# A delta-rule attention block and a GELU feed-forward in one kernel: small steps move between ScalarE, GpSimd, VectorE and the DMA queues

## The chip, the cores and the metric

The kernel runs on one core of a Trainium2 chip. A core has TensorE (matrix products into PSUM), VectorE, ScalarE and GpSimd (called DVE, ACT and POOL in the profile) and SyncE (SP), which here only issues DMAs. Each engine works through its own queue in order and waits on semaphores where it needs another's result. The metric is the device time of one execution in microseconds; the kernel before has a median of 678.57 us in 6 runs (676.61 to 679.24).

## The reference, cut to what matters

```python
# batch 4, heads 8, seq 768, head dim 48; everything float32
k_n = k / (norm(k) + 1e-6)
for t in range(seq):
    y[t]  = q[t] @ state                       # read before the update
    v_old = k_n[t] @ state
    state = state + beta[t] * outer(k_n[t], v[t] - v_old)

x   = y as (4*768, 8*48)                       # 3072 tokens of 384
h   = x @ w_in                                 # 384 -> 2048
out = (0.5 * h * (1 + erf(h / sqrt(2)))) @ w_out   # 2048 -> 384
```

`w_in` and `w_out` arrive as float64 (a division by a NumPy square root made them so); the kernel turns them into float32 itself.

## The kernel before, in words

**Tiling.** The sequence is cut into 12 chunks of 64 steps. A chunk is held as two units (`a` = 0, 1), each with two batches on the two halves of the 128 partitions and 8 heads along the free side. A unit's number within a pair of chunks is `u.t` = 0 to 3; `first` are the four units of chunks 0 and 1, `third` the two of chunk 2, `fourth` the two of chunk 3.

**Attention.** Within a chunk the recurrence becomes a triangular system per head. For a pair of chunks ("group" 0 holds chunks 0 and 1, group 1 chunks 2 and 3, and so on) the kernel

- squares K and sums per head (`squares`, L272), takes the root (`root` for group 0, a power instruction on GpSimd in `prep`, L303, later) and makes factors from beta and the norm (`factors`, L264; `finish_both`, `finish`);
- forms products of K with K (`grams`, `diagonals`) and of Q with K (`queries`; for chunks from 2 on VectorE applies the causal mask while it reads PSUM, L396);
- inverts the 32 by 32 diagonal blocks on VectorE: a scaled mask XM on GpSimd (L423), a flip (L428, L429), some 30 elimination steps (L436, L438), and transposes back (L447, L451);
- joins the 32 blocks into blocks of 64 on TensorE in two levels (`join`, `join_run`, L511), with VectorE scaling level 0 (L519) and ScalarE copying level 1 (L523).

Then each chunk in turn is put against the state (psK, L566; W, L574), solved (psU), used (psY) and transposed to `xT` for the feed-forward. V is multiplied by K's norm first (`scale_v`, L326, on GpSimd).

**Feed-forward.** A chunk has 16 blocks of the first layer (`fc1`: psH, L671; GELU on ScalarE, L673). The second layer is psO (L684) with a copy on ScalarE (L688) and two output DMAs from ScalarE's queue (L678) for chunks 0 and 1, and a scheme with fewer products (L709) for the others. psH and psO share two PSUM banks (tag `mlp`), so a psH has to wait until the GELU, or the psO copy, two before it has read its bank. The tag `dn` has two buffers as well, which psG, psJ, psK, psU and psY take in the order in which the program asks for them.

**Weights.** The 16 parts of `w_in` and `w_out` are unpacked from float64 bits by five VectorE instructions each (`begin`, `mantissas`, `signed`: L219 to L237) with one exponent pass on ScalarE (`exponents`, L224). The raw bits wait in memory that is used otherwise later.

**Order.** Up to L899 the order on every engine is written by hand. After that each step has a plan time: chunk c's feed-forward lies from c + 1 to c + 2, and the other steps are put at times between (`at`, L790). All are sorted by plan time and emitted. VectorE executes in exactly that order; for the other engines a planner goes through the emitted instructions with estimated costs, and takes the earliest emitted one that is ready when an engine is free. What it decides is fixed in the program; on the chip each engine executes its list in order.

**What the change touches.** The beta DMAs (L163, on GpSimd's queue) and K's and Q's first loads (L152, L155); the hand-written loop over `first` (L823 to L830) with beta's transposes (`signs`, L802); `squares` and `prep` (L272 to L303), where chunks 2 and 3 take one ScalarE instruction per head with an accumulated sum (L280); `scale_v` (L325); the zeroing of `Kb`, a padded K buffer of later chunks (L911); and plan times in L920 to L935. `Kb` lies in the memory of the closed start pool, so it can be written only after the last unpacking.

Of the kernel before, what the change touches and what calls it, by code (L numbers as in the profile page):

```python
# [8 lines left out]
F32 = mybir.dt.float32  # L9
# [3 lines left out]
ACT = mybir.ActivationFunctionType  # L13
# [3 lines left out]
def kernel(  # L17
# [133 lines left out]
    for u in first:  # L151
        fetch_in(u.Kp[:, :, 0:D], k, u, (nc.sync, nc.scalar))  # L152
    bt = w_in_sb.rearrange("q g m f -> q (g m f)")[0:B * H, 0:2 * S].rearrange(
        "n (c p t) -> n c p t", p=2, t=C)
    for u in first:  # L155
        fetch_in(u.Qp[:, :, 0:D], q, u)
# [6 lines left out]
    for p in range(2):  # L163
        nc.gpsimd.dma_start(out=bt[:, :, p, :],
                            in_=beta.rearrange("b h (c t) -> (b h) c t", t=C))
# [106 lines left out]
    def squares(u, n, engine=None):  # L272
        kd = u.Kn[:, :, 0:D]
        if engine is nc.gpsimd:
            ksq = su.tile([128, H, D], F32, tag="w_e", name="ksq")
        else:
            ksq = wk.tile([128, H, D], F32, tag="ksq", name="ksq")
        if engine is None and u.c < 4:
            for h in range(H):
                nc.scalar.activation(ksq[:, h], kd[:, h], ACT.Square, accum_out=n[:, h:h + 1])  # L280
            return
        if engine is None:
            nc.scalar.activation(ksq, kd, ACT.Square)
        else:
            engine.tensor_tensor(ksq, kd, kd, op=ALU.mult)
        nc.vector.tensor_reduce(n, ksq, axis=AX.X, op=ALU.add)  # L286

    def prep(c):
        us = [tiles[c, a] for a in range(NA)]
        g = c // 2  # L290
        if c % 2 == 0:
            new_group(g)
        if c == 2:
            n23 = wk.tile([128, 2 * NA, H], F32, tag="n0", name="n0", bufs=1)
            ns[2], ns[3] = n23[:, 0:NA], n23[:, NA:]
            ns["both"] = n23
        elif c > 3:
            ns[c] = wk.tile([128, NA, H], F32, tag="n", name="n", bufs=4)
        n = ns[c]
        for u in us:  # L300
            squares(u, n[:, u.a])
        flat = n.rearrange("q a h -> q (a h)")
        nc.gpsimd.tensor_tensor(flat, flat, half, op=ALU.pow)  # L303
# [21 lines left out]
    def scale_v(u, engine=nc.gpsimd):  # L325
        engine.tensor_tensor(u.V, u.V, ns[u.c][:, u.a].unsqueeze(2).to_broadcast([128, H, D]),  # L326
                                op=ALU.mult)
# [495 lines left out]
    for u in first:  # L823
        squares(u, n0[:, u.t], nc.gpsimd if u.t % 2 else nc.vector)
        transposed(u, (0,))
        if u.t > 0:
            diagonals(first[u.t - 1])
        if u.t == 2:
            signs(0, 2)
# [75 lines left out]
    def late():  # L905
        start.close()
        more.append(ctx.enter_context(tc.tile_pool(name="late", bufs=1)))
        small[0] = ctx.enter_context(tc.tile_pool(name="few", bufs=1, space=bass.MemoryType.PSUM))
        for a in range(NA):
            Kb = more[0].tile([128, 2, NP, 2, HB], F32, name=f"Kb{a}")  # L910
            nc.gpsimd.memset(Kb, 0.0)  # L911
            for c in range(5, NC, 2):
                tiles[c, a].Kb = Kb
# [6 lines left out]
    plan += [at(0.99, 1.0, [(1.0, prep, 2)]), at(1.65, 1.655, [(1.0, finish_both)]), at(2.75, 2.76, [(1.0, finish, 4)]), at(2.45, 2.46, [(1.0, queries, third)]),  # L920
             at(1.12, 1.6, state_steps(1)), at(1.45, 1.46, [(1.0, prep, 3)]),
             at(1.75, 2.45, eliminate_steps(1)),
             at(2.58, 2.74, join_steps(1)), at(2.72, 2.98, state_steps(2)),
             at(2.6, 2.61, [(1.0, prep, 4)]), at(2.8, 2.9, [(1.0, grams, [tiles[4, a] for a in range(NA)])])]
# [3 lines left out]
    for c in range(4, NC):  # L928
# [5 lines left out]
        t = c - (2.1 if c % 2 == 0 else 2.6) if c > 5 else {4: 2.1, 5: 2.62}[c]  # L934
# [62 lines left out]
```

## Time and profile before

| what | value |
|---|---|
| median of 6 runs | 678.57 us (676.61 to 679.24) |
| the profiled execution | 681.93 us |
| its span, first to last instruction | 679.9 us |
| mean granted TensorE clock | 0.975 |
| TensorE busy (matmul) | 647.5 us, 95% |
| VectorE busy | 450.9 us, 66% |
| ScalarE busy | 220.9 us, 32% |
| GpSimd busy | 90.2 us, 13% |
| share of TensorE in the chain that ended last | 75% |

How to read it: times in the profile count from the span's start. A row of a timeline has the start in us, the duration in us, the engine, the source line, the operation, output and inputs by their names in the program, the shapes, how often (x24: 24 neighbours merged), and in brackets how long the engine had been idle before and what released it. "issue" stands for a wait that the profile can't put down to anybody. PEld is TensorE loading weights, which overlaps its matmuls. A float32 matmul appears as two instructions, so a block of psH is six.

### The profile page before, as it was taken

The numbers are of one execution on the slowest core, as the hardware profiler recorded it, in microseconds if no ns is written. First come the engines' busy times: TensorE is split into PE (matmuls) and PEld (weight loads), VectorE is DVE, ScalarE is ACT, GpSimd is POOL, SyncE is SP. The second block draws the span as 40 slices with busy tenths as digits, with TensorE's granted clock in tenths as the row PEclk, the third lists the DMA queues.
The fourth block names the chain that finished last, engine by engine and source line by source line (L and its number), as shares of the span: only waits on it lengthen the run. The fifth ranks groups of instructions, "written<-read, shape, count | busy, mean of one in ns | idle before, by whom it ended". The sixth has DMA issues, their size and how long they took to land.

```text
span 679.9 us, 21674 instructions
## 1 busy us (share of the span) xinstructions
PE 647.5 (95%) x9542; PEld 564.6 (83%) x9542; DVE 450.9 (66%) x920; ACT 220.9 (32%) x571; POOL 90.2 (13%) x91
## 2 busy tenths in 40 slices
PE   6867999998999999999999999999999999999997
PEld 4655875775689988989989989989989989989996
DVE  5999899895589865569856569856569844324021
ACT  3357654212443033233142233142142133132220
POOL 5051300402211012111021111021111010000000
PEclk9976799997999999999999999999999999999999
DMA  9785646202532142421233421221301210100101
GB/s 129 182 239 171 121 122 174 47 0 44 89 46 40 40 54 52 68 52 26 50 44 54 71 47 25 48 27 28 58 13 25 53 20 3 24 2 2 23 1 25
DMA packets 157566, 39.75 MB, mean 58 GB/s; under 512 B 149216, under 2 KB 152288, under 8 KB 157472
## 3 DMA queue, kind: packets, MB, share of 16 engines
q1 hardware_dynamic: 151424, 33.06, 25.5%
q10 hardware_dynamic: 5952, 5.12, 3.4%
q8 instruction: 75, 1.23, 0.8%
q0 software_dynamic: 96, 0.20, 0.1%
q14 instruction: 19, 0.16, 0.1%
HBM read 33.62 MB, written 4.72 MB: 56 GB/s over the span
## 4 chain that ended last, share of the span: by engine, by line
PE 75%; DVE 5%; issue 1%; POOL 0%; ACT 0%
PE psH L671 31%; PE psY L709 12%; PE psX L709 12%; PE psZ L709 4%; PE psJ L511 3%; PE psK L566 3%; PE psG L361 3%; PE psO L684 2%; PE psU L591 2%; DVE tmp L436 2%; PE psY L609 2%; DVE Nu L438 2%; PE psY L618 1%; PE psX L653 1%; DVE u L754 0%
## 5 line engine op out<-in xcount | busy, mean ns | idle before, releaser
L671 PE MATMUL psH<-xT,w_in_sb 128*128 128x256 f32 x1152 | 264.0, 386 | 3.9 <-ACT G L673 3.2
L671 PEld LDWEIGHTS psH<-xT,w_in_sb 128*128 128x128 f32 x1152 | 217.8, 192 | 35.7 <-ACT G L673 4.4
L673 ACT ACTIVATE G<-psH 128x256 f32<-128x256 f32 x192 | 73.3, 383 | 189.7 <-PE psH L671 177.8
L438 DVE TENSOR_TENSOR Nu<-Nu,tmp 128x30 f32<-128x30 f32 (+9 forms) x180 | 62.3, 346 | 6.2
L436 DVE TENSOR_TENSOR tmp<-Nu 128x30 f32<-128x30 f32 (+9 forms) x180 | 61.6, 342 | 5.1
L709 PE MATMUL psY<-w_out_sb,G 128*128 128x192 f32 x320 | 57.0, 329 | 1.1 <-DVE u L754 0.4
L709 PE MATMUL psX<-w_out_sb,G 128*128 128x192 f32 x320 | 56.2, 329 | 0.0
L709 PEld LDWEIGHTS psY<-w_out_sb,G 128*128 128x128 f32 x320 | 51.7, 190 | 2.8 <-DVE u L754 2.5
L709 PEld LDWEIGHTS psX<-w_out_sb,G 128*128 128x128 f32 x320 | 52.2, 190 | 0.7
L684 PE MATMUL psO<-w_out_sb,G 128*128 128x384 f32 x128 | 47.3, 512 | 0.2 <-DVE w_out_sb L237 0.2
L654 ACT COPY xT<-psX 128x384 f32<-128x384 f32 x24 | 11.4, 478 | 106.7 <-PE psX L653 105.5
L303 POOL TENSOR_TENSOR n<-n,half 128x16 f32<-128x16 f32 x10 | 29.4, 2941 | 92.6 <-DVE n L286 69.1
L597 ACT COPY U<-psU 64x192 f32<-64x192 f32 x96 | 30.0, 313 | 19.6 <-PE psU L591 18.4
L396 DVE TENSOR_TENSOR P<-psG,mask 128x1024 f32<-128x1024 f32 x10 | 12.3, 1228 | 35.9 <-PE psG L361 35.9
L684 PEld LDWEIGHTS psO<-w_out_sb,G 128*128 128x128 f32 x128 | 23.7, 196 | 14.1 <-DVE w_out_sb L237 0.9
L326 POOL TENSOR_TENSOR V<-V,n 128x384 f32<-128x384 f32 x22 | 22.0, 1009 | 95.3 <-DMA V<-in_v_dram 41.6
L574 DVE TENSOR_TENSOR W<-psK,V 128x384 f32<-128x384 f32 x22 | 12.2, 552 | 33.4 <-ACT y L573 33.4
L460 POOL MEMSET Zf<- 32x512 f32 x23 | 12.4, 540 | 153.5 <-DVE Zf L451 125.0
L718 DVE TENSOR_TENSOR S<-G 128x512 f32<-128x512 f32 x20 | 13.8, 688 | 25.8 <-ACT G L673 25.7
L632 DVE TENSOR_TENSOR x<-psY,y 64x192 f32<-64x192 f32 x80 | 28.2, 353 | 0.9
L709 PE MATMUL psY<-T,G 128*128 128x192 f32 x160 | 28.2, 329 | 0.0
L709 PE MATMUL psX<-T,G 128*128 128x192 f32 x160 | 28.1, 329 | 0.0
(135 smaller groups left out, 860.5 us busy)
## 6 DMA issues: line engine op xcount, KB each, us to landing
Kp<-in_k_dram SPq DMA_DIRECT2D x76, 96.0 KB, 3.5
w_out_sb<-in_moe_w_in_dram SPq DMA_DIRECT2D x24, 256.0 KB, 3.9
V<-in_v_dram SPq DMA_DIRECT2D x48, 96.0 KB, 2.9
out_dram<-o_sb ACTq DMA_DIRECT2D x48, 96.0 KB, 2.2
w_raw<-in_moe_w_out_dram SPq DMA_DIRECT2D x10, 384.0 KB, 4.3
Zf<-in_moe_w_out_dram SPq DMA_DIRECT2D x6, 384.0 KB, 4.4
Qp<-in_q_dram SPq DMA_DIRECT2D x64, 32.0 KB, 2.1
Qp<-in_q_dram SPq DMA_DIRECT2D x16, 96.0 KB, 4.6
```

Source lines behind the costliest of these rows:

```text
L303: nc.gpsimd.tensor_tensor(flat, flat, half, op=ALU.pow)
L326: engine.tensor_tensor(u.V, u.V, ns[u.c][:, u.a].unsqueeze(2).to_broadcast([128, H, D]), op=ALU.mult)
L361: nc.tensor.matmul(psG[HALF[p], r, i * NP + j, :], lhsT=u.Kt[rows, p, j, :], rhs=(u.Qt if x else u.Kt)[rows, p, j, :], start=True, stop=True)
L436: nc.vector.tensor_tensor(tmp, nu[:, j + 1:, j:j + 1].to_broadcast([128, n, j]), nu[:, j:j + 1, 0:j].to_broadcast([128, n, j]), op=ALU.mult)
L438: nc.vector.tensor_tensor(nu[:, j + 1:, 0:j], nu[:, j + 1:, 0:j], tmp, op=ALU.add)
L511: nc.tensor.matmul(psJ[to, i, :], lhsT=(xm if level else off)[rows, u, :], rhs=zf[rows, u, HB:C] if level else xm[rows, u, :], start=True, ...
L597: copy(pairs(u.U[HALF[p]], s), u.psU[HALF[p ^ s], p])
L632: nc.vector.tensor_tensor(dst, src, pairs(u.y[HALF[p ^ s]], s), op=ALU.add)
L671: nc.tensor.matmul(psH, lhsT=w_in_sb[:, f // 2, m, f % 2 * 128:(f % 2 + 1) * 128], rhs=xTs[c][:, m, :], start=(m == 0), stop=(m == NM - 1))
L673: nc.scalar.activation(G[:, f, :], psH, ACT.Gelu)
L684: nc.tensor.matmul(u.psO, lhsT=G[:, f, u.a * 128:(u.a + 1) * 128], rhs=w_out_sb[:, f, :], start=(f == 0), stop=(f == NF - 1))
L709: nc.tensor.matmul(ps_, lhsT=lhs[:, f, :], rhs=rhs[:, f, :], start=first and f == 0, stop=f == FH - 1, skip_group_check=not first)
```

## The change

- **Beta.** Its two DMAs go to SyncE's queue, behind K and ahead of Q, instead of GpSimd's.
- **The hand-written start.** The squares of unit 3 are done by VectorE instead of GpSimd; `diagonals` of unit 2 comes after the loop; beta's transposes (`signs(0, 2)`) come after it instead of after unit 2's transposes.
- **Squares of chunks 2 and 3.** The same 32 ScalarE instructions, formerly inside `prep(2)` (plan time 0.99) and `prep(3)` (1.45), are single steps with plan times from 1.08 to 1.5. Both `prep`s, now holding only the power instruction for these chunks, are at 1.51.
- **V of chunks 2 and 3.** Eight ScalarE multiplies per unit, one per head with the norm as a scale per partition, instead of one GpSimd instruction per unit.
- **Kb.** Zeroed by ScalarE (a mask times 0.0) instead of a GpSimd memset.
- **Plan times around the joins of group 1.** The masked queries of chunk 2 move from 2.45 to 2.675 and `prep(4)` from 2.6 to 2.67, both behind the second of the three joins (2.58 to 2.74); `finish(4)` moves from 2.75 to 2.97; the load of chunk 5's K from 2.62 to 2.69.

```diff
     for u in first:
         fetch_in(u.Kp[:, :, 0:D], k, u, (nc.sync, nc.scalar))
...
+    for p in range(2):
+        nc.sync.dma_start(out=bt[:, :, p, :], in_=beta.rearrange("b h (c t) -> (b h) c t", t=C))
     for u in first:
         fetch_in(u.Qp[:, :, 0:D], q, u)
...
-    for p in range(2):
-        nc.gpsimd.dma_start(out=bt[:, :, p, :],
-                            in_=beta.rearrange("b h (c t) -> (b h) c t", t=C))
...
-        if engine is None and u.c < 4:
-            for h in range(H):
-                nc.scalar.activation(ksq[:, h], kd[:, h], ACT.Square, accum_out=n[:, h:h + 1])
-            return
...
+    def sum_of_squares(u, h):
+
+        if "both" not in ns:
+            n23 = wk.tile([128, 2 * NA, H], F32, tag="n0", name="n0", bufs=1)
+            ns[2], ns[3] = n23[:, 0:NA], n23[:, NA:]
+            ns["both"] = n23
+        if h == 0:
+            u.ksq = wk.tile([128, H, D], F32, tag="ksq", name="ksq")
+        nc.scalar.activation(u.ksq[:, h], u.Kn[:, h, 0:D], ACT.Square,
+                             accum_out=ns[u.c][:, u.a, h:h + 1])
...
     def scale_v(u, engine=nc.gpsimd):
+        if u.c in (2, 3):
+            for h in range(H):
+                nc.scalar.mul(u.V[:, h], u.V[:, h], ns[u.c][:, u.a, h:h + 1])
+            return
...
     for u in first:
-        squares(u, n0[:, u.t], nc.gpsimd if u.t % 2 else nc.vector)
+        squares(u, n0[:, u.t], nc.gpsimd if u.t == 1 else nc.vector)
         transposed(u, (0,))
-        if u.t > 0:
-            diagonals(first[u.t - 1])
-        if u.t == 2:
-            signs(0, 2)
+        if u.t in (1, 2):
+            diagonals(first[u.t - 2 + 1])
+    diagonals(first[2])
+    signs(0, 2)
     diagonals(first[3])
...
-            nc.gpsimd.memset(Kb, 0.0)
+            nc.scalar.mul(Kb.rearrange("q p j h n -> q (p j h n)"),
+                          low.rearrange("q a b -> q (a b)")[:, 0:NP * 4 * HB], 0.0)
...
-    plan += [at(0.99, 1.0, [(1.0, prep, 2)]), at(1.65, 1.655, [(1.0, finish_both)]), at(2.75, 2.76, [(1.0, finish, 4)]), at(2.45, 2.46, [(1.0, queries, third)]),
-             at(1.12, 1.6, state_steps(1)), at(1.45, 1.46, [(1.0, prep, 3)]),
+    sums = [(1.0, sum_of_squares, tiles[c, a], h) for c in (2, 3) for a in range(NA) for h in range(H)]
+    plan += [at(1.08, 1.5, sums), at(1.51, 1.511, [(1.0, prep, c) for c in (2, 3)]), at(1.65, 1.655, [(1.0, finish_both)]), at(2.97, 2.971, [(1.0, finish, 4)]), at(2.675, 2.676, [(1.0, queries, third)]),
+             at(1.12, 1.6, state_steps(1)),
...
-             at(2.6, 2.61, [(1.0, prep, 4)]), at(2.8, 2.9, [(1.0, grams, [tiles[4, a] for a in range(NA)])])]
+             at(2.67, 2.671, [(1.0, prep, 4)]), at(2.8, 2.9, [(1.0, grams, [tiles[4, a] for a in range(NA)])])]
...
-        t = c - (2.1 if c % 2 == 0 else 2.6) if c > 5 else {4: 2.1, 5: 2.62}[c]
+        t = c - (2.1 if c % 2 == 0 else 2.6) if c > 5 else {4: 2.1, 5: 2.69}[c]
```

## The prediction

> **What bounds the kernel now.** I read the page's rows of busy time first, then busy time by stretch (cut where the work changes its kind), then each engine's own timeline around the edits. The stretches, with their columns PE, PEld, DVE, ACT, POOL, clock, DMA share, GB/s:
>
> ```profile
> PE 647.5 (95%) x9542; PEld 564.6 (83%) x9542; DVE 450.9 (66%) x920; ACT 220.9 (32%) x571; POOL 90.2 (13%) x91
> ```
>
> ```profile
> 0.00:43.00 43.00, 30.62 (x721) 25.38 (x723) 33.72 (x94) 18.66 (x38) 11.83 (x26) 0.96 0.88 195
> ...
> 96.00:123.50 27.50, 27.08 (x158) 16.61 (x157) 26.91 (x39) 10.29 (x20) 2.49 (x4) 1.00 0.58 153
> 123.50:187.00 63.50, 57.74 (x810) 41.59 (x809) 43.89 (x97) 18.14 (x43) 13.96 (x12) 0.95 0.28 48
> 187.00:680.00 493.00, 487.22 (x7005) 443.70 (x7003) 298.73 (x630) 138.39 (x344) 47.34 (x40) 1.00 0.21 35
> ```
>
> TensorE is busy 487 of the last 493 us and waits for nobody there, so what the change wins or loses before 187 us arrives at the end one for one. Up to 121 us VectorE is the bound: it unpacks the weights (L219 to L237), 26.91 of 27.50 us busy, and the second matmul of chunk 0 (psO) can't run ahead of the last unpacked part. From 123 to 187 the two take turns.
>
> **Squares of chunks 2 and 3 (ScalarE).** TensorE's timeline:
>
> ```profile
> 64.20 1.56 PE L671 MATMUL psH<-xT,w_in_sb 128*128 128x256 f32 x6
> 67.95 1.61 PE L671 MATMUL psH<-xT,w_in_sb 128*128 128x256 f32 x6 [2.19 <-ACT G L673]
> ...
> 71.35 7.81 PE L671 MATMUL psH<-xT,w_in_sb 128*128 128x256 f32 x24
> ...
> 81.10 5.45 PE L671 MATMUL psH<-xT,w_in_sb 128*128 128x256 f32 x24
> ```
>
> Thirteen squares run from 64.6 to 67.5 on ScalarE ahead of the first GELU; both psH banks are full, and TensorE idles 2.19 us. Then the same 24 matmuls take 7.81 instead of 5.45 us, and the 64 small ones of L478 1.92 instead of 1.20: half clock, 2.4 + 0.7 = 3.1 us. Given late plan times the squares yield to a GELU that is ready; a GELU then waits for one square (0.23 us each). I count the bubble and the half clock after it as gone: TensorE is 2.2 + 3.1 = 5.3 us ahead at 79 us.
>
> Here a rule weighs in. The Trainium skill, "TensorE: Matmul & The Clock Gate", section "HAM oscillation", lets the clock fall only after idle gaps above about 3.4 us. By it a gap of 2.19 us costs itself alone, the slow stretch stays, and the stall that I find below has no clock penalty. The row says otherwise: a fresh gap of 2.19 us, then half speed. Over this trace, a stretch of 3.4 us that is about half idle is followed by slow matmuls; 1.47 us of idle at 150.6 was not. I take the row.
>
> What is this worth? TensorE may not overtake the unpacking. VectorE, though, twice waits for others in this stage, and a third time just after it:
>
> ```profile
> 80.88 0.56 DVE L574 TENSOR_TENSOR W<-psK,V 128x384 f32<-128x384 f32 x1 [2.26 <-ACT y L573]
> ...
> 91.81 0.96 DVE L236 SCALAR_TENSOR_TENSOR w_e<-Zf,w_e 128x768 uint32<-128x768 uint32 x1 [1.10 <-ACT w_e L224]
> ...
> 125.49 1.83 DVE L429 TENSOR_TENSOR Nu<-Nu,XM 128x1024 f32<-128x1024 f32 x1 [1.62 <-POOL XM L423]
> ```
>
> The first waits for psK, which follows seven blocks of psH on TensorE; 5.3 us earlier, the wait of 2.2 is gone. The second is an exponent pass (L224) queued behind eight copies of U (2.6 us); with TensorE ahead these come before the pass is due: 1.1. So the unpacking ends **3.3 us** earlier; 1.7 if the half clock stayed, and near nothing if ScalarE were late elsewhere. The other 2 us of TensorE's lead turn into idle, harmlessly. Both power instructions (L303, 2.9 us each) on POOL move behind the last square; the norms are wanted at 120.7, so even a delay of 15 us is covered.
>
> **Start.** POOL loses two beta DMAs (1.44 us), SP gains them behind K: at its 0.7 us per issue, 1.4 us for every later load on SP (Q, V, w_in, next K and Q). I find at least 2 us between landing and use for each, so this is free; without that cover it is 1.4. The beta transfer (96 packets between 4.2 and 7.4 us) leaves K's transfers alone, the last tile's squares go to VectorE (0.55 us instead of a wait of 1.29 for POOL), and the beta transposes move one tile later. VectorE's root starts up to 1.1 us sooner, but the flip of the diagonals needs the last diagonal, which TensorE's stall of 1.14 us at 12.4 holds. Between 0 and 1.1 I take **0.5**.
>
> **V and Kb leave POOL.** POOL's timeline:
>
> ```profile
> 121.01 1.00 POOL L911 MEMSET Kb<- 128x512 f32 x2 [38.60 <-PE psG L361]
> 121.96 1.63 POOL L326 TENSOR_TENSOR V<-V,n 128x384 f32<-128x384 f32 x2
> 123.53 1.92 POOL L423 TENSOR_TENSOR XM<-low,gt 128x1024 f32<-128x1024 f32 x1
> ```
>
> Without the first two, XM starts at 122.0, and VectorE's elimination 1.5 us earlier.
>
> But ScalarE now does two zeroings (the row of L458, half a microsecond apart: 1.1) and 16 multiplies for chunk 2, with plan times below those of the copies of psO (L688). All become ready at the end of the unpacking, D; L688 only 1.6 us later, so ScalarE is taken. A multiply of 128x48: the square's row says 0.23, its start-to-start without the accumulator's read 0.14 is the lower end. The Trainium skill, "ScalarE: Activation LUTs", section "What ACT_TABLE_LOAD costs", adds about 93 ns for a scale read per partition, and lets neighbours overlap by as much: an estimate of 0.32 each, 0.23 apart. I take 0.23: 3.6 us (2.2 to 5.1). With 0.14 the sum would end 1.4 us lower.
>
> ```profile
> 122.46 0.48 ACT L688 COPY o_sb<-psO 128x384 f32<-128x384 f32 x1 [5.86 <-PE psO L684]
> ...
> 123.55 2.75 PE L671 MATMUL psH<-xT,w_in_sb 128*128 128x256 f32 x12
> 127.02 5.23 PE L671 MATMUL psH<-xT,w_in_sb 128*128 128x256 f32 x23 [0.71 <-ACT G L673]
> ```
>
> L688 starts at D + 4.9 instead of D + 1.6; behind it in ScalarE's queue stand the output DMAs and the first GELUs, and psH of chunk 1 has no bank before the copy. The second psH pair, and all after it, starts **3.3 us** later relative to D. About 2.7 of it is one gap, over half of a 3.4 us stretch: by the reading above half clock follows, **2.5 us** of matmul time. Chunk 3's 16 multiplies rank below the GELUs and fill gaps of 0.9 us between them.
>
> **Joins in front of the mask.** The same place on VectorE, then on TensorE:
>
> ```profile
> 155.27 1.25 DVE L396 TENSOR_TENSOR P<-psG,mask 128x1024 f32<-128x1024 f32 x1
> 156.39 1.04 DVE L286 TENSOR_REDUCE n<-ksq 128x8 f32<-128x384 f32 x2
> 157.46 1.39 DVE L519 TENSOR_TENSOR XM<-psJ,gm 32x512 f32<-32x512 f32 x2
> ```
>
> ```profile
> 156.57 0.24 PE L511 MATMUL psJ<-XM,G 32*32 32x32 f32 x2 [0.56 <-DVE P L396]
> 158.95 0.23 PE L511 MATMUL psJ<-Zf,XM 32*32 32x32 f32 x1 [2.13 <-issue]
> ```
>
> L519 moves ahead of 2.0 us of work, so with the 1.5 above it comes 3.5 us earlier. The late "issue" wait ends 0.1 us after L519, which frees its PSUM bank: a wait on VectorE. The 128 query matmuls (psG, 1.1 us), now in the gaps of 113 to 121, move here and add 1.1.
>
> From 127.0 to 186.3 (chunk 2's first psH) TensorE takes 59.3 us. Of it 1.47 + 0.56 + 2.13 + 0.27 + 0.62 = 5.05 are idle, and 1.9 half clock after 158 (four psO take 2.93, two 1.39, where two take 0.91 later). Pure work 52.4, plus 1.1: 53.4. With VectorE's chain ahead it runs unbroken: 3.3 + 2.5 + 53.4 = 59.2. This stretch thus gains **0.1**; five microseconds of idle are spent on the stall. Moving finish(4), prep(4), a K load (four issues on SP, between block loads) by some hundredths of a chunk happens while VectorE has gaps of 5 and 8 us: nothing, and at worst their own 1.8 us.
>
> **Sum.** 0.5 + 3.3 + 0.1 = 3.9 us. The profiled execution took 681.93 (span 679.9, 2.0 around it), so 678.0 in its terms; on the median 678.57, **674.7**. A measurement of this kernel can tell about 0.2%, 1.4 us, from no change.
>
> **Rivals.**
> - *No stall for chunk 1, or a short one without half clock.* For it: the stall rests on an order that the planner decides and on a price no row shows exactly. With the stall and full clock 2.5 us less: 672.2. With no stall, TensorE waits 0.9 us for the joins, and the stretch ends 4.2 earlier: 670.6. Middle 671.5.
> - *The unpacking keeps its pace.* ScalarE then delays the exponents behind squares: gain only 0.5 + 0.1, 678.0: no change. Against it: L224 has 3.8 us from L219 to L236, and squares are short.
> - *Slower: ScalarE's multiplies hold psH.* If the 32 multiplies of both chunks stand ahead of L688 at 0.32 us each (10.2 + 1.3), it starts 9.9 us later: 6.6 beyond my sum, 681.3. It decides from a shift of 3.3 + 3.9 = 7.2 us. Against it: chunk 3's plan times (2.6) lie above L688's (1.9).
>
> **Chances.** My sum 0.44; no or little stall 0.32; unpacking unchanged 0.10; slower 0.14. So faster 0.76, same 0.10, slower 0.14. The range, 670.0 to 680.0, reaches over the first three and the unknown price of a multiply, and leaves the last out.
>
> **What would show it.** Right: no wait of psH for a GELU near 66, 24 psH in 5.5 us after it; L574 without a wait; the last L237 of the unpacking at about 117; L429 straight behind L428; 16 ScalarE multiplies ahead of L688, then a TensorE gap over 2 us and slow psH; no gap over 1 us at the joins. Wrong: L688 ahead of the multiplies (faster), the last L237 still at 120 (no gain), or beta's transposes waiting for their DMA and the elimination starting later than 17.2.

## The result, and the profile after

The changed kernel takes 675.75 us (median of 15 runs, 674.35 to 677.19) against 678.85 us of the kernel before in the same session (34 runs, 676.27 to 679.5): a ratio of 0.996, 95% interval 0.995 to 0.997. That is 3.1 us faster; 674.7 was predicted. The profiled execution took 675.75 us with a span of 674.0. The total came out nearly as forecast. The terms of its sum did not, and the rest of this text is about that: that the sum fits is in part luck.

From here on four marks cut the span: the first psH of chunk 0, the end of the unpacking (the end of the last L236 on VectorE, called D as in the prediction), the first psH of chunk 1, the first psH of chunk 2. Each row is one profiled execution, in us; the last columns are the timed runs.

| kernel | first psH | to D | D to psH of chunk 1 | to psH of chunk 2 | to the end | span | median (runs) | ratio to before, interval |
|---|---|---|---|---|---|---|---|---|
| before | 60.70 | 60.11 | 2.74 | 62.78 | 493.54 | 679.9 | 678.85 (34) | |
| before_again | 60.38 | 58.51 | 2.74 | 61.43 | 493.54 | 676.6 | 678.89 (20) | 1.0001 (0.9989 to 1.0013) |
| **after** | 59.37 | 57.31 | 5.25 | 57.68 | 494.41 | 674.0 | 675.75 (15) | 0.9960 (0.9950 to 0.9970) |
| after_again | 59.46 | 57.31 | 5.25 | 57.40 | 495.15 | 674.6 | 676.08 (6) | 0.9967 (0.9951 to 0.9983) |
| squares_only | 60.72 | 57.33 | 2.74 | 60.35 | 493.55 | 674.7 | 677.41 (22) | 0.9979 (0.9967 to 0.9990) |
| squares_back | 60.48 | 57.34 | 5.25 | 56.12 | 494.67 | 673.9 | 675.26 (6) | 0.9954 (0.9936 to 0.9972) |
| squares_block | 59.62 | 60.10 | 5.25 | 57.39 | 494.75 | 677.1 | 675.71 (22) | 0.9961 (0.9948 to 0.9974) |
| start_back | 60.28 | 57.32 | 5.25 | 56.39 | 494.19 | 673.4 | 676.69 (22) | 0.9972 (0.9963 to 0.9981) |
| v_back | 59.44 | 57.31 | 2.74 | 60.31 | 494.44 | 674.2 | 675.61 (6) | 0.9959 (0.9943 to 0.9975) |
| v_late | 60.06 | 57.32 | 2.74 | 57.84 | 494.48 | 672.5 | 673.76 (6) | 0.9939 (0.9924 to 0.9954) |
| v_more | 59.37 | 57.32 | 8.86 | 58.30 | 494.89 | 678.7 | 679.97 (17) | 1.0026 (1.0015 to 1.0037) |
| finish_early | 59.04 | 57.29 | 5.25 | 57.41 | 493.31 | 672.3 | 673.83 (6) | 0.9946 (0.9930 to 0.9961) |
| joins_back | 60.49 | 57.30 | 5.25 | 56.15 | 493.32 | 672.5 | 673.49 (6) | 0.9936 (0.9921 to 0.9951) |
| v_behind | 59.73 | 57.32 | 2.74 | 59.91 | 493.32 | 673.0 | 674.88 (5) | 0.9942 (0.9927 to 0.9957) |

Medians come from several sessions, so kernels are best compared by their ratio to the kernel before, which ran beside each. The runs of one kernel lie up to 5.7 us apart (before_again, 676.37 to 682.02), and the two profiles of the kernel before differ by 3.3 us of span, all of it ahead of chunk 2; most of that goes with the half clock that is looked at below.

The two profiles nearest to their medians, before_again (678.68 us) and after (675.75), show where the 2.9 us between them arise: 1.0 ahead of the first psH, 1.2 more up to D, 1.2 more up to chunk 2, 0.9 lost behind it, and 0.3 outside the span. The last was not in the forecast, which counted 2.0 us around the span for both kernels: in all runs of the kernel before and of squares_only it is 2.0 to 2.1 us, in all runs of the changed kernel 1.7 to 1.8. Start_back, squares_block, v_back and joins_back stay at 1.7 to 1.8 as well, so which part brings it is open.

Busy time by stretch, in the changed kernel (columns as in the prediction), and below it the stretch of the kernel before that answers to the first row:

```profile
66.00:92.00 26.00, 24.85 (x465) 20.67 (x464) 24.84 (x36) 18.82 (x77) 6.18 (x2) 1.00 0.54 118
92.00:119.60 27.60, 25.77 (x93) 15.03 (x91) 27.01 (x39) 12.66 (x29) 1.60 (x1) 1.00 0.57 151
119.60:180.00 60.40, 56.94 (x872) 42.19 (x873) 42.27 (x96) 23.66 (x69) 9.81 (x9) 0.97 0.26 44
180.00:674.00 494.00, 487.82 (x7006) 443.81 (x7004) 300.51 (x631) 138.63 (x344) 46.65 (x40) 1.00 0.21 36
```

```profile
68.00:96.00 28.00, 27.68 (x464) 23.21 (x465) 24.12 (x35) 18.16 (x65) 5.99 (x2) 0.88 0.48 104
```

VectorE is still the bound up to 117 us (27.01 of 27.60), TensorE behind 180. The clock column is what changed most: 1.00 instead of 0.88 in the stretch from 66 to 92, and 0.97 instead of 0.95 in the one from 119.6 to 180, where one drop is left.

**Squares.** TensorE's timeline around the first GELUs:

```profile
62.66 1.56 PE L678 MATMUL psH<-xT,w_in_sb 128*128 128x256 f32 x6
65.65 1.56 PE L678 MATMUL psH<-xT,w_in_sb 128*128 128x256 f32 x6 [1.43 <-ACT G L680]
...
68.82 2.86 PE L678 MATMUL psH<-xT,w_in_sb 128*128 128x256 f32 x12
72.18 2.86 PE L678 MATMUL psH<-xT,w_in_sb 128*128 128x256 f32 x12 [0.50 <-ACT G L680]
...
76.98 5.45 PE L678 MATMUL psH<-xT,w_in_sb 128*128 128x256 f32 x24
```

The bubble is smaller, 1.43 us instead of 2.19, but still there: ScalarE runs five squares and two exponent passes ahead of the first GELU. No half clock follows it: 12 psH take 2.86 us, and 24 take 5.45. On VectorE:

```profile
77.32 0.56 DVE L581 TENSOR_TENSOR W<-psK,V 128x384 f32<-128x384 f32 x1
...
87.70 0.96 DVE L235 SCALAR_TENSOR_TENSOR w_e<-Zf,w_e 128x768 uint32<-128x768 uint32 x1 [0.58 <-ACT w_e L223]
...
119.95 1.23 DVE L436 TENSOR_TENSOR Nu<-Nu,XM 128x1024 f32<-128x1024 f32 x1 [0.24 <-POOL XM L430]
```

L581 (L574 before) waits no more, the exponent's wait has shrunk from 1.10 to 0.58, and the elimination waits 0.24 for XM instead of 1.62.

**The stall.** ScalarE at the end of the unpacking, and TensorE after it:

```profile
116.76 1.15 ACT L918 ACTIVATE Kb<-low 128x512 f32<-128x512 f32 x2 [4.29 <-DVE n L265]
117.82 3.70 ACT L331 ACTIVATE V<-V,n 128x48 f32<-128x48 f32 x16
121.43 0.83 ACT L695 COPY o_sb<-psO 128x384 f32<-128x384 f32 x2
121.91 2.50 ACTq L685 DMA_DIRECT2D out_dram<-o_sb  x4
```

```profile
121.93 22.67 PE L678 MATMUL psH<-xT,w_in_sb 128*128 128x256 f32 x96 [2.35 <-ACT o_sb L695]
```

and the same place in squares_back, a variant with the same stall:

```profile
123.08 21.36 PE L678 MATMUL psH<-xT,w_in_sb 128*128 128x256 f32 x96 [2.35 <-ACT o_sb L695]
```

Two zeroings, sixteen multiplies (3.70 / 16 = 0.231 us each), and then the copies of psO at D + 4.75. TensorE idles 2.35 us. The 96 matmuls of chunk 1 then take 22.67 us; in squares_back, without half clock, they take 21.36. In the changed kernel's profile the granted clock is 0.50 from 121.95 to 125.37 us, and in that time a matmul starts every 0.43 us instead of every 0.22.

**The joins.** TensorE before, TensorE after, and VectorE after:

```profile
152.04 1.20 PE L511 MATMUL psJ<-XM,G 32*32 32x32 f32 x64 [1.47 <-DVE XM L447]
```

```profile
149.69 1.20 PE L518 MATMUL psJ<-XM,G 32*32 32x32 f32 x64
```

```profile
150.94 1.40 DVE L526 TENSOR_TENSOR XM<-psJ,gm 32x512 f32<-32x512 f32 x2 [2.03 <-PE psJ L518]
154.91 1.39 DVE L526 TENSOR_TENSOR XM<-psJ,gm 32x512 f32<-32x512 f32 x2 [2.58 <-PE psJ L518]
```

The direction of the wait has turned. Before, TensorE waited here 1.47, 0.56 and 2.13 us for VectorE; now VectorE waits for TensorE.

**A new wait.** VectorE, and then TensorE, some microseconds into chunk 2:

```profile
178.15 0.67 DVE L268 TENSOR_TENSOR gm<-beta_m,r 128x16 f32<-128x16 f32 x1
178.86 0.75 DVE L269 TENSOR_TENSOR gm<-gm,r 128x16 f32<-128x16 f32 x1
179.53 1.75 DVE L702 TENSOR_TENSOR T<-w_out_sb 128x1536 f32<-128x1536 f32 x1
...
184.78 1.30 DVE L353 STREAM_TRANSPOSE Kt<-Kb 128x512 f32<-128x512 f32 x2
```

```profile
185.54 0.34 PE L368 MATMUL psG<-Kt 48*64 48x64 f32 x8 [0.91 <-DVE Kt L353]
```

finish(4) (L265 to L269) now stands in front of the sums of w and the transposes Kt, and TensorE waits 0.91 us for Kt. The part from chunk 2 to the end, 493.54 us before, takes 494.41.

### The profile page after: what moved, and what is told of

The parts are those of the page before. It is cut to its first block, busy times and chain, and to the rows that moved or that the text cites. A ratio compares the mean times of both kernels' runs of the same rounds, so it can differ in the third digit from the quotient of the medians.

```text
span 674.0 us, 21703 instructions
## 1 busy us (share of the span) xinstructions
PE 641.3 (95%) x9542; PEld 559.4 (83%) x9542; DVE 452.3 (67%) x921; ACT 229.1 (34%) x605; POOL 82.0 (12%) x82
## 3 DMA queue, kind: packets, MB, share of 16 engines
q8 instruction: 75, 1.23, 0.8%
## 4 chain that ended last, share of the span: by engine, by line
PE 77%; DVE 14%; ACT 3%; issue 3%; DMA 2%; POOL 0%; SPq 0%; ACTq 0%; DVEq 0%; POOLq 0%
PE psH L678 33%; PE psY L716 12%; PE psX L716 11%; PE psZ L716 3%; PE psJ L518 3%; PE psK L573 3%; PE psG L368 3%; PE psO L691 3%; DVE Nu L445 3%; DVE tmp L443 3%; PE psU L598 2%; PE psY L616 1%; DVE w_e L235 1%; DMA Kp<-in_k_dram 1%; DVE w_out_sb L236 1%
## 5 line engine op out<-in xcount | busy, mean ns | idle before, releaser
L691 PE MATMUL psO<-w_out_sb,G 128*128 128x384 f32 x128 | 45.1, 495 | 1.6 <-DVE w_out_sb L236 1.6
L581 DVE TENSOR_TENSOR W<-psK,V 128x384 f32<-128x384 f32 x22 | 12.2, 553 | 28.7 <-ACT y L580 28.7
L333 POOL TENSOR_TENSOR V<-V,n 128x384 f32<-128x384 f32 x18 | 17.1, 955 | 104.8 <-DMA V<-in_v_dram 82.6
L526 DVE TENSOR_TENSOR XM<-psJ,gm 32x512 f32<-32x512 f32 x20 | 13.8, 690 | 23.2 <-PE psJ L518 23.1
```

The source lines that it names most:

```text
L691: nc.tensor.matmul(u.psO, lhsT=G[:, f, u.a * 128:(u.a + 1) * 128], rhs=w_out_sb[:, f, :], start=(f == 0), stop=(f == NF - 1))
```

## The experiments

Three questions were put: what the squares are worth, what the multiplies on ScalarE and the moved joins are worth together, and what the small moves cost.

### The two kernels again

before_again and after_again are the two kernels unedited.

> The kernel before, once more, for a second profile. The profiled execution that the prediction was summed against took 681.9 us, 3 us above the median, and had half clock after 66 and after 156 us. Theory A: how long TensorE is at half clock differs from execution to execution, and the first profile was an unlucky one; this one shows 676 to 679 us, and at least one of the two half-clock stretches shorter or gone. Theory B: profiling itself adds 3 us; then this one takes about 682 again, with both stretches as they were.

> The changed kernel as it is, beside the three below on one chip. 675.2 to 676.2 by every theory; its profile shows whether the half clock that followed the stall of 2.35 us (psH x96 in 22.67 us instead of 21.36) is there again: theory A (the phase of the clock's 3.4 us stretches decides it) allows either, theory B (the gap's length decides) asks for it again.

Measured: 678.89 and 676.08 us (ratios 1.0001 and 0.9967). before_again's profile has a span of 676.6 instead of 679.9, with the same instructions: 1.6 us less to D and 1.35 less between the chunks. There the bubble was 2.40 us, yet VectorE's wait for psK only 0.5 us instead of 2.2: the granted clock was halved for 3.4 us, where in the first profile it was halved for 6.8. At the joins the same holds: 3.4 us at half clock instead of 6.8. So the profile that the prediction was made from had caught two of the kernel's dearer cases in one execution, as theory A has it. after_again has the stall of 2.35 us and the psH x96 of 22.67 us again.

### Squares alone, on the kernel before

```diff
-at(0.99, 1.0, [(1.0, prep, 2)]), ... at(1.45, 1.46, [(1.0, prep, 3)]),
+at(1.08, 1.5, sums), at(1.51, 1.511, [(1.0, prep, c) for c in (2, 3)]),
```

> The kernel before with the squares part of the change alone. Theory A (the gain of the unpacking comes from the squares): the wait of L574 for psK (2.2 us) goes, the last unpacking ends 2.2 to 2.8 us earlier, the stall of psH at chunk 1's start doesn't come, and the execution takes 2 to 3 us less than before. Theory B (the unpacking is earlier for other reasons, such as the start): under 0.7 us less.

Measured: 677.41 us, ratio 0.9979 (0.9967 to 0.9990), some 1.4 us. To D it takes 57.33 us; behind D the work is that of the kernel before, with 3.4 us at half clock. Neither expectation held in full: there is a gain, and it is less than half of the one forecast. Its fastest runs are no faster than those of the kernel before (676.4 against 676.3 us); what changed is how often a run is dear, here one of over 678.7 us: 18 of the 34 runs of the kernel before, and 4 of the 22 of squares_only.

### Squares back, within the change

squares_back gives the changed kernel's 32 square steps the old plan times, so that thirteen stand in a row ahead of the first GELU again; squares_block restores the old code as well (two groups of sixteen inside prep).

```diff
 squares_back
-at(1.08, 1.5, sums), at(1.51, 1.511, [(1.0, prep, c) for c in (2, 3)]),
+at(0.99, 1.0, sums[:16] + [(0.01, prep, 2)]), at(1.45, 1.46, sums[16:] + [(0.01, prep, 3)]),
 squares_block
-at(1.08, 1.5, sums), at(1.51, 1.511, [(1.0, prep, c) for c in (2, 3)]),
+at(0.99, 1.0, [(1.0, prep, 2)]), ... at(1.45, 1.46, [(1.0, prep, 3)]),
```

> The changed kernel with the squares of chunks 2 and 3 at their old plan times, inside the two power steps. Theory A: the unpacking ends 2.2 to 2.8 us later, 2 to 3 us more than the changed kernel, so about the time before. Theory B (TensorE hides it elsewhere): within 0.7 us of the changed kernel.

> The changed kernel with the squares of chunks 2 and 3 exactly as before: two groups of sixteen inside prep, planned at 0.99 and 1.45. Theory A (the prediction: thirteen squares in a row ahead of the first GELU cost VectorE two waits): from the first psH to the end of the unpacking 58.5 to 60.1 us as in the two profiles of the kernel before, instead of 57.3, and 1.2 to 2.8 us more, 677.0 to 678.5. Theory B (the row of squares costs nothing by itself, only the half clock that may follow it does, and whether it follows is decided by where the gap falls): 57.3 us in a profile without half clock after 65 us, and a median less than 1.0 us above the changed kernel's.

Measured: 675.26 us (0.9954) and 675.71 us (0.9961), the changed kernel's time within what can be told. Their profiles, TensorE first of squares_back, then of squares_block:

```profile
67.74 1.56 PE L678 MATMUL psH<-xT,w_in_sb 128*128 128x256 f32 x6 [1.49 <-ACT G L680]
69.23 1.20 PE L485 MATMUL psJ<-Zf,XM 32*32 32x32 f32 x64
70.36 5.79 PE L678 MATMUL psH<-xT,w_in_sb 128*128 128x256 f32 x24
```

```profile
66.88 2.01 PE L674 MATMUL psH<-xT,w_in_sb 128*128 128x256 f32 x6 [2.39 <-ACT G L676]
68.82 1.92 PE L481 MATMUL psJ<-Zf,XM 32*32 32x32 f32 x64
70.66 7.41 PE L674 MATMUL psH<-xT,w_in_sb 128*128 128x256 f32 x24
```

and VectorE of squares_block:

```profile
79.80 0.56 DVE L577 TENSOR_TENSOR W<-psK,V 128x384 f32<-128x384 f32 x1 [2.27 <-ACT y L576]
...
90.74 0.96 DVE L235 SCALAR_TENSOR_TENSOR w_e<-Zf,w_e 128x768 uint32<-128x768 uint32 x1 [1.14 <-ACT w_e L223]
```

The profile of squares_block shows the whole of the prediction's mechanism: a gap of 2.39 us, half clock, VectorE's two waits of 2.27 and 1.14, and 60.10 us to D. But that execution took 678.84 us, and among the 22 runs only four lie there (678.8 to 679.2); the other eighteen lie between 674.6 and 676.5, like the changed kernel's. In squares_back the same thirteen squares stand in a row and cost nothing: a gap of 1.49, no half clock, no wait for psK, 57.34 us to D. The gap is shorter because TensorE came to it later: the clock, halved since 43 us, was granted in full only at 63.9 us, 3.4 us behind the first psH, and in squares_block (halved since 44 us) at 61.0, 1.4 us behind it. So the price is in the half clock, not in the squares, and it falls due in a minority of the runs. This fits theory B of the second expectation; that the four runs are those with the half clock is argued from the one profiled among them. It also goes some way to explain why squares_only gained 1.4 us while undoing the same part within the change loses nothing that can be told: a median doesn't see four dear runs of 22, but it does see 18 of 34. Why dear runs are rarer within the change stays open.

### V and Kb back on GpSimd

```diff
-            nc.scalar.mul(Kb.rearrange("q p j h n -> q (p j h n)"), ..., 0.0)
+            nc.gpsimd.memset(Kb, 0.0)
...
-        if u.c in (2, 3):
-            for h in range(H):
-                nc.scalar.mul(u.V[:, h], u.V[:, h], ns[u.c][:, u.a, h:h + 1])
-            return
```

> The changed kernel with V of chunks 2 and 3 and the zeroing of Kb back on GpSimd. Theory A (this part costs more than it brings: a stall of 2.35 us and about 1.2 us of half clock at chunk 1's start, against 1.5 us for XM on a VectorE chain that has 2 us to spare): no stall, XM 1.5 us later, 1 to 2.5 us less than the changed kernel. Theory B (the earlier XM is worth its 1.5 us): 1 to 1.5 us more than the changed kernel.

Measured: 675.61 us (0.9959): the same as the changed kernel, as neither theory had it. The stall is gone (2.74 us from D), but XM is late again, and TensorE pays at the joins:

```profile
147.95 1.38 PE L514 MATMUL psJ<-XM,G 32*32 32x32 f32 x64 [2.14 <-DVE XM L450]
149.26 4.29 PE L687 MATMUL psO<-w_out_sb,G 128*128 128x384 f32 x8
```

Eight psO take 4.29 us instead of 2.85: half clock after the wait. A stall of 2.35 us in front of chunk 1 and a wait of 2.14 us at the joins change places, each with its own half clock.

### V later on ScalarE, and more of it sooner

v_late plans V of chunk 2 at 2.1 to 2.4 and the zeroings of Kb at 2.03; v_more loads and scales V of chunk 3 together with that of chunk 2.

```diff
 v_late
-at(max(c - 0.4, 1.66), c - 0.3, v_steps(c))
+at(2.1 if c == 2 else c - 0.4, 2.4 if c == 2 else c - 0.3, v_steps(c))
 v_more
-at(max(c - 0.4, 1.66), c - 0.3, v_steps(c))
+at(1.66 if c == 3 else max(c - 0.4, 1.66), 1.7 if c == 3 else c - 0.3, v_steps(c))
-at(c - 1.0, c - 0.99, [(1.0, load_v, c)])
+at(1.62 if c == 3 else c - 1.0, 1.63 if c == 3 else c - 0.99, [(1.0, load_v, c)])
```

> The changed kernel (675.75) with the 16 multiplies of V of chunk 2 planned behind the copies of psO instead of ahead of them, into the gaps between GELUs, and the two zeroings of Kb a step of their own at 2.03. Theory A (the stall of 2.35 us ahead of chunk 1's first psH is paid in full until VectorE's lead of 2.0 us at the joins, 150.94, is used up): the stall goes, the joins' waits on VectorE shrink to nothing, psH of chunk 1 comes 2.4 us earlier, and the time falls by 2.0 to 2.6 us, to 673.1 to 673.8. Theory B (the stall and a wait at the joins are exchanged one for one, as with V and Kb on GpSimd, where the joins' wait of 2.14 us came back): within 0.6 us of the changed kernel, with a TensorE wait of about 2 us at the joins.

> The changed kernel with V of chunk 3 loaded at 1.62 and scaled at 1.66, so that 32 multiplies instead of 16 stand ahead of the copies of psO: the prediction's slower rival, at the measured 0.231 us each. Theory A (the lead of VectorE at the joins is used up, so every further microsecond of the stall arrives at the end): the stall grows from 2.35 to 6.05 us, and the time rises by 3.7 us, with a longer half clock up to 5.0: 679.4 to 680.8. Theory B (slack remains behind the stall): less than 2 us more, under 677.8.

Measured: v_late 673.76 us, 0.9939 (0.9924 to 0.9954), v_more 679.97 us, 1.0026 (1.0015 to 1.0037). Theory A held for v_more, and in the main for v_late, whose gain over the changed kernel is 1.4 to 1.9 us by the ratios. In v_late the first copy comes between multiplies, at D + 1.65, the matmuls of chunk 1 follow it at full clock, and VectorE no longer waits for TensorE at the first join (ScalarE, TensorE, VectorE):

```profile
118.53 0.55 ACT L331 ACTIVATE V<-V,n 128x48 f32<-128x48 f32 x2
119.04 0.48 ACT L695 COPY o_sb<-psO 128x384 f32<-128x384 f32 x1
```

```profile
120.13 21.17 PE L678 MATMUL psH<-xT,w_in_sb 128*128 128x256 f32 x96
```

```profile
149.64 1.39 DVE L526 TENSOR_TENSOR XM<-psJ,gm 32x512 f32<-32x512 f32 x2
```

The multiplies between GELUs cost nothing: the 96 psH take 21.17 us, as in squares_back (21.36). Of the 2.5 us of stall and 1.3 of half clock, 1.7 come back at the joins (57.84 us between the chunks against squares_back's 56.12), where VectorE's lead is used up: TensorE waits 0.60 and 0.28 us, and the matmuls between L526 and the mask, which follow VectorE step by step, take the rest. v_more on TensorE:

```profile
125.54 23.08 PE L678 MATMUL psH<-xT,w_in_sb 128*128 128x256 f32 x96 [5.95 <-ACT o_sb L695]
```

Sixteen more multiplies, 3.6 us more stall (8.86 instead of 5.25 from D), and 3.9 us more time than after_again beside it (679.97 against 676.08). Nothing is left to cover a longer stall. This is the prediction's slower rival, 1.3 us below the price that it gave (681.3): a multiply cost 0.231 us and not 0.32, which is 2.8 us for 32 of them, and the changed kernel beside it took 1.4 us more than the forecast.

### finish(4) and the joins

finish_early plans finish(4) at 2.75 again; joins_back, on top of it, the queries, prep(4) and the K load of chunk 5 at their old times.

```diff
 both
-at(2.97, 2.971, [(1.0, finish, 4)])
+at(2.75, 2.76, [(1.0, finish, 4)])
 joins_back
-at(2.675, 2.676, [(1.0, queries, third)]) ... at(2.67, 2.671, [(1.0, prep, 4)]) ... 5: 2.69
+at(2.45, 2.46, [(1.0, queries, third)]) ... at(2.6, 2.61, [(1.0, prep, 4)]) ... 5: 2.62
```

> The changed kernel with the scale factors of chunk 4, finish(4), planned at 2.75 again, as in the kernel before. Theory A (they stand in front of the sums of w and of the transposes Kt, so that TensorE waits 0.91 us ahead of psG at 184.6): that wait goes, the stretch from chunk 2's first psH to the end takes 493.5 us again instead of 494.4, and the time falls by 0.9 us, to 674.9. Theory B (VectorE has no room for them earlier either, their 1.8 us delay the joins or the first psH of chunk 2): no gain, 675.4 to 676.2.

> finish_early with the queries of chunk 2, prep(4) and the K load of chunk 5 at their old plan times too (2.45, 2.6, 2.62): the query mask and its 128 matmuls stand in front of the joins again. Theory A (VectorE is 2.0 us ahead of TensorE at the joins since the stall holds TensorE, so the mask's 1.3 to 2.0 us are covered, and 1.1 us of psG leave the stretch from chunk 1's to chunk 2's first psH): 0.4 to 1.1 us less than finish_early. Theory B, the prediction's (the joins come 3.5 us later and TensorE waits for them again): 0.5 to 1.5 us more than finish_early.

Measured: 673.83 us (0.9946) and 673.49 us (0.9936). The wait in front of psG is gone from finish_early's TensorE timeline, and the last part takes 493.31 us:

```profile
183.51 0.56 PE L368 MATMUL psG<-Kt 48*64 48x64 f32 x20
```

Its own finish(4) ran at 160 us, in one of VectorE's idle stretches:

```profile
160.79 0.17 DVE L269 TENSOR_TENSOR gm<-gm,r 128x16 f32<-128x16 f32 x1
```

By the table the move cost 1.1 us (494.41 against 493.31), in after_again 1.8; by the ratios the undoing gains 0.9 to 1.4 us, with intervals that overlap those of the changed kernel. Theory A's 0.9 is at the lower end. Moving the joins behind the mask again costs nothing: the mask fits into VectorE's lead exactly.

```profile
149.86 1.20 DVE L403 TENSOR_TENSOR P<-psG,mask 128x1024 f32<-128x1024 f32 x1
...
152.00 1.39 DVE L526 TENSOR_TENSOR XM<-psJ,gm 32x512 f32<-32x512 f32 x2
```

joins_back needs 56.15 us between the chunks, squares_back, with the joins in front and also without half clock, 56.12. Theory B's wait of TensorE at the joins did not come; a gain, 0.3 us by the medians, can't be told from none.

This and v_back belong together. Before, VectorE was late at the joins; the change lets it come earlier in two ways, by taking V and Kb off GpSimd and by moving the joins in front of the mask. Undoing either alone costs nothing that can be told, since the other still covers the wait. Both undone together were not tried within the change. An estimate from the ratios: from squares_only to the changed kernel it is 1.3 us (0.9979 less 0.9960), of which the start gives 0.3 to 0.8 and finish(4) takes 0.9 to 1.4, so that 1.4 to 2.4 us are left for the two together, the 0.3 outside the span among them.

### The start

```diff
-    for p in range(2):
-        nc.sync.dma_start(out=bt[:, :, p, :], in_=beta...)
+        nc.gpsimd.dma_start(out=bt[:, :, p, :], in_=beta...)
-        squares(u, n0[:, u.t], nc.gpsimd if u.t == 1 else nc.vector)
+        squares(u, n0[:, u.t], nc.gpsimd if u.t % 2 else nc.vector)
```

(and diagonals and signs in their old order)

> The changed kernel with beta's two transfers on GpSimd's queue again, the squares of the last tile of the start on GpSimd and the diagonals and signs in their old order. Theory A (the first psH came 1.3 us earlier, 59.37 instead of 60.70, by this part alone, and the whole kernel behind it moves with it): the first psH at 60.4 to 60.7, and 0.9 to 1.3 us more, 676.6 to 677.0. Theory B (the start scatters with K's landing by as much, as one run with the new start and a first psH at 60.48 suggests): within 0.4 us of the changed kernel.

Measured: 676.69 us (0.9972), 0.3 to 0.8 us above the changed kernel, by the ratios of its two measurements (0.9972 less 0.9967 or 0.9960, times 678 us). The first psH came at 60.28. Over all profiles it lies at 60.28 to 60.72 with the old start (four) and at 59.04 to 60.49 with the new one (ten), means 60.52 and 59.71: 0.8 us. The intervals of the ratios overlap, so the profiles carry this more than the times do. Theory A named the cause and put its size too high; the scatter of theory B is real too.

### A version meant to beat both

v_behind leaves V on GpSimd, but behind XM, by way of a copy of the norms that VectorE makes once its elimination runs; Kb is zeroed on ScalarE, and finish(4) is at 2.75.

```diff
+    def late_n():
+        ns["late"] = more[0].tile([128, 2 * NA, H], F32, name="late_n")
+        nc.vector.tensor_copy(ns["late"], ns["both"])
+    plan = [at(1.9, 1.901, [(1.0, late_n)])]
...
+        n = ns["late"][:, (u.c - 2) * NA:(u.c - 1) * NA] if u.c in (2, 3) else ns[u.c]
```

> A version meant to beat both: the changed kernel with V of chunks 2 and 3 on GpSimd again but behind XM (VectorE copies the 32 norms of 0.2 us first, after its elimination has begun, and V is scaled by the copy), the zeroing of Kb left on ScalarE, and finish(4) at 2.75. Theory A (with no stall VectorE's elimination is the bound up to the joins, as its one idle wait at the joins of v_late says): chunk 1's first psH 2.74 us behind the unpacking, TensorE waits 1 to 2 us at the joins, 57.6 to 58.0 us from chunk 1's to chunk 2's first psH, 493.3 us from there, 672.3 to 672.9. Theory B (TensorE bounds that stretch, and the multiplies between GELUs cost v_late 1.2 us of it): no wait at the joins over 0.5 us, 56.2 to 56.8 us, 671.0 to 671.8.

Measured: 674.88 us, 0.9942 (0.9927 to 0.9957). The wait at the joins is theory A's, the time isn't. There is no stall and no late XM; TensorE arrives at the joins, waits, and is then slowed:

```profile
147.90 1.20 PE L515 MATMUL psJ<-XM,G 32*32 32x32 f32 x64 [1.80 <-DVE XM L451]
...
149.03 4.54 PE L688 MATMUL psO<-w_out_sb,G 128*128 128x384 f32 x8
```

The wait of 1.80 us brought 1.69 us of half clock (4.54 against 2.85). v_late waits there 0.60 us. The difference is made on GpSimd and VectorE (in this order):

```profile
124.67 3.44 POOL L330 TENSOR_TENSOR V<-V,late_n 128x384 f32<-128x384 f32 x4 [4.39 <-DMA Kb<-in_k_dram]
```

```profile
124.39 0.32 DVE L440 TENSOR_TENSOR tmp<-Nu 128x150 f32<-128x150 f32 x1
124.74 0.93 DVE L442 TENSOR_TENSOR Nu<-Nu,tmp 128x150 f32<-128x150 f32 x1
125.71 0.84 DVE L440 TENSOR_TENSOR tmp<-Nu 128x168 f32<-128x168 f32 x1
```

While GpSimd multiplies V, four steps of the elimination take 0.84 to 0.93 us instead of 0.32 to 0.35. From L433 to the transpose XM<-Nu the elimination takes 25.43 us; it takes 23.30 in the changed kernel, and 24.4 in the kernel before and in v_back, where L429 (1.83 us in the prediction's row, 1.23 in the changed kernel) and the step behind it run beside V. GpSimd in the kernel before:

```profile
125.40 2.61 POOL L326 TENSOR_TENSOR V<-V,n 128x384 f32<-128x384 f32 x2
```

So moving V to ScalarE took 1.1 us off VectorE's chain, besides the 1.4 by which XM comes earlier. The four kernels v_late, finish_early, joins_back and v_behind can't be told apart; v_late with finish(4) at 2.75 wasn't tried.

## Why the prediction was right, and where it wasn't

The forecast of 3.9 us was 0.8 above the measured 3.1. The exchange of a stall in front of chunk 1 for the waits at the joins was forecast and came. But two of the three terms were far off, in opposite directions, a move put at nothing cost a microsecond, and 0.3 us came from outside the span. That these errors nearly cancel is luck. No part undone alone gives the 3.1 us back: the most is the start's 0.8. How the gain divides is therefore known from profiles and from the subtraction above, not from a run for each term.

**Start: 0.5 forecast, 0.8 by the profiles and 0.3 to 0.8 by the ratios.** Right, and by the limit that was named: the flip of the diagonals did remain a limit in part; in seven of the ten profiles with the new start it waits 0.18 to 0.97 us for the last diagonal.

**Squares: 3.3 forecast; nothing that can be told when undone within the change, 1.4 when done alone.** The step that failed is "I count the bubble and the half clock after it as gone": the bubble stayed at 1.43, and the half clock does not follow in every run of the old order (squares_back). The waits named (2.2 for psK, 1.1 for the exponent) are right for the execution profiled; to D it took 60.11, and the changed kernel takes 57.31, so 2.8 of 3.3 were seen there. From before_again it is 1.2, from squares_back 0. The term was sized by one execution's clock and set against the median of many.

**V, Kb and joins: 0.1 forecast, 1.2 to 2.9 by the profiles of the two kernels, 1.4 to 2.4 by the subtraction above** (D to chunk 2's first psH: 65.5 and 64.2 before, 62.9 and 62.7 after; one profile of squares_only, which has none of these moves, is at 63.1, so a single execution says little). Where the multiplies would stand, 0.23 us each, the gap (2.7; 2.35 measured) and the start of the copies (D + 4.9; 4.75) were right, and v_more confirms the price of the stall. Three sizes were wrong. The half clock after it costs 1.3 us (22.67 against 21.36), not 2.5, and was absent in three of the seven profiles with this stall; 3.4 us at half speed can't cost more than 1.7. Second, the second psH pair is not 3.3 us later: before, it had its own wait of 0.71 for a GELU behind ScalarE's two separate copies and their output DMAs; now both copies run together and the second pair follows at once, some 1.9 us later than before where the clock is full (D + 8.2 in squares_back, D + 6.2 and 6.4 in the kernel before). Third, VectorE reaches the joins 2.5 us sooner by V and Kb alone, not 1.5: the transpose XM<-Nu starts 26.6 us behind D, before 29.1, 1.1 of it by the contention with GpSimd that v_behind shows. The joins then run without a wait, as forecast, with 2.03 us to spare, and so, with V and Kb moved, their place in front of the mask gained nothing, as joins_back shows.

**finish(4), "nothing, and at worst their own 1.8 us": 0.9 to 1.6 us lost.** The cover named, gaps of 5 and 8 us on VectorE, ends at 173.7 us; at 2.97 the step lands behind it, at 177.7, and ahead of L702 and L353. What is late next, Kt and with it TensorE, should have been followed. The step also releases GpSimd's multiply of V, which then ran beside it (from 177.96 for 1.61 us): L268 and L269 took 0.67 and 0.75 us instead of 0.17. The Trainium skill, "GPSIMD Engine Reference", section "Specifications", says that GpSimd shares its SBUF interfaces with VectorE and contends with instructions that read two SBUF inputs. These two do, and so do the steps of v_behind's elimination; the rows agree, and the prediction had left it out.

**The rule weighed.** The Trainium skill's limit of about 3.4 us of idle ("TensorE: Matmul & The Clock Gate", section "HAM oscillation") did not hold here: only one gap in the table below is longer, and in 12 other cases half clock followed too. Taking the row was right. The same page, section "What's actually happening", says that the stretches over which the clock is decided run freely and do not start with the kernel. The traces agree: between 60 and 190 us each change of the granted clock lies on a grid of 3.41 us, and where the grid lies differs from profile to profile. So what counts may be how much of a gap falls into one step of the grid, and the third column gives that:

| TensorE's gap, us | where | idle in one step of the grid, us | half clock in the next step |
|---|---|---|---|
| 5.95 | ahead of chunk 1: v_more | 3.39 | 1 of 1 |
| 2.35 | ahead of chunk 1: after, after_again, finish_early, squares_block | 2.35 | 4 of 4 |
| 2.35 | ahead of chunk 1: squares_back, start_back, joins_back | 1.21, 1.76, 1.85 (the gap lies across a border) | 0 of 3 |
| 2.19 to 2.40 | at the first GELUs: before, before_again, squares_block | 2.04 to 2.40 | 3 of 3 |
| 1.80, 2.14 | at the joins: v_behind, v_back | 1.80, 2.14 | 2 of 2 |
| 0.56 and 2.13 or 2.14 | at the joins: before, before_again | 1.82, 2.36 | 2 of 2 |
| 1.38 | at the joins: squares_only (eight psO then take 4.54 us) | 1.38 | 1 of 1 |
| 1.47, 1.27 | at the joins: before, before_again | 0.79, 1.03 | 0 of 2 |
| 1.04 to 1.49 | at the first GELUs: after, after_again, v_more, finish_early, squares_only, v_late, squares_back | 1.00 to 1.43 | 0 of 7 |

In these profiles 2.04 us and more of idle in one step were always followed by half clock, 1.37 us and less never; between 1.38 and 1.85 both occur. Why the halving lasts one step in some profiles and two in others (before, squares_block) stays open.

**Rivals.** "No stall" (671.5) did not happen; v_late shows what it is worth, 1.4 to 1.9 us by the ratios and not the 3.2 between the two forecasts, because VectorE's lead at the joins, 2.0 us, is all that can be had. "Slower" is v_more, at 679.97 us on the other side of no change, as worked out. "The unpacking keeps its pace" did not happen: ScalarE did not delay the exponents, whose wait shrank from 1.10 to 0.58, and up to D it took 57.3 us in every profile with the new order, against 60.1 and 58.5 in the kernel before. For the median, though, the squares are worth between its nothing and the forecast's 3.3.

## What to carry to other kernels

Before a stall's removal is counted, find who is second: here the stall in front of chunk 1 and the wait at the joins stood in for each other, and a part was worth something only once the other engine had no lead left. Two moves that cure the same wait cost nothing when undone one at a time; undo them together as well. Where one gap brings a lower clock, profile the kernel twice before its price goes into a sum against a median. A small step moved "into a gap" has to be looked up at its new place, with what stands behind it in the queue.

## What was not expected of the hardware

The same gap of 2.35 us was followed by half clock in four profiles and by full speed in three, worth 1.3 us each: the four had it within one step of a 3.41 us grid that does not start with the kernel, the three across a border. That this is why a kernel's runs scatter by 3 us and more, although its instructions are fixed, is likely but shown only for the profiled executions. And a multiply on GpSimd, off every chain, made the VectorE steps beside it 2.5 to 2.9 times as long (0.86 / 0.35 and 0.93 / 0.32); it cost VectorE's elimination for chunks 2 and 3 1.1 us in the kernel before, and 2.1 in v_behind.
